# Attention and an MLP mixer in one kernel: value banks as two tiles, idle matmuls in the first steps, one weight load moved behind an input load

## The chip, the cores and the metric

One core of one Trainium2 chip runs the kernel. A core has TensorE (PE, matrix multiplication, writing into PSUM), VectorE (DVE), ScalarE (ACT), GpSimd (POOL) and SyncE (SP), which all work through their own instruction queues and wait for one another through semaphores. Sixteen DMA engines move data between the chip's memory (HBM) and the on-chip SBUF. PSUM has eight banks of 2 KB on each of 128 partitions. The metric is the device time of one execution in microseconds (us); lower is better.

## The reference

Batch 8, 12 heads, 448 rows, head size 64. First an attention with squared ReLU in place of softmax, then a mixer with a token part and a channel part.

```python
scores = scale * np.matmul(q, k.transpose(0, 1, 3, 2))
attn = np.maximum(scores, 0.0) ** 2 / S
x = (attn @ v).transpose(0, 2, 1, 3).reshape(B, S, H * D)      # 8 x 448 x 768
h = np.maximum(x.transpose(0, 2, 1) @ w_tok1, 0.0) @ w_tok2    # 448 -> 256 -> 448
u = x + h.transpose(0, 2, 1)
out = u + np.maximum(u @ w_ch1, 0.0) @ w_ch2                   # 768 -> 1536 -> 768
```

## The kernel before, in words

The work is cut into 24 groups, numbered i: four heads of one batch each, three groups to a batch (DB = 3). The order of all instructions is written out by hand.

For each group, `load_four` brings q, k and v by DMA from POOL's queue, with a cast to bf16: six DMAs of 112 KB (two for each of q, k, v). The pool for these has four buffers for each name. `transposes(i)` turns q and k with 56 small matmuls into a PSUM tile of two banks, which is copied to `qkT` (L148). `scores(i, c)`, c from 0 to 6, makes four matmuls of 64x64 by 448 columns into `sc_ps` (L159), and ACT writes their ReLU as `at` (L168). `square` squares `at` on DVE (L175). `values(i, cs)` adds up the products with v in `acc_ps` (L187). `values_out` scales the two halves of `acc_ps` into `xT` (L205 on DVE, and where `split` is set L201 on ACT for the second half).

Then the mixer: `x_back(i)` turns `xT` into `x_sb`, for the first six groups by matmuls into `x_ps` (L230) and a copy (L240, L241, L243), from group 6 on (XDMA = 6) by two DMA transposes on SP's queue (L223). `token1` multiplies `x_sb` with w_tok1 (`t_ps`, L252, ReLU L260), `token2` with w_tok2 (`h_ps`, L276), and DVE adds `xT` to give `uT_sb` (L284). `u_back` turns this back with DMA transposes on SP's queue (L306). `channel1` (L318, ReLU L325) and `channel2` (L357, sum L364) are cut into units that stand in a queue.

PSUM is shared by three pools: `ps_att` has two slots of two banks, taken in turn by `sc_ps` and by `qkT_ps` in the first groups ("att"); `ps_acc` has one slot of two banks ("acc") for `acc_ps`, later also for `qkT_ps` and `h_ps`; `ps_mm` has two slots of one bank ("bank") for everything else. One slot of two banks is one tile: instructions of two engines that use different halves of it are ordered one after the other.

The first three groups (steps 0 to 2) are a loop over c in which transposes, scores and values of neighbouring groups alternate (L438 to L465). Then comes a stretch for i = 3 written out by hand (L468 to L497), in which the first channel matmuls begin (`channel1_begin`, L336). From i = 4 on a loop (L500) does for each i: scores of group i, values of group i - 1, `x_back`, loads for group i + 3, transposes of group i + 1, `token1`, `token2`; in between, `fill(share)` takes channel units from the queue as a credit allows. From group 10 on, a load waits on POOL for the transposes of an earlier `x_sb` (`gate`, L518).

The loads stand in POOL's queue in the order in which they are written. Eight DMAs can be open at a time: POOL stops at a load until the one eight places before it has landed. The weights w_ch1 and w_ch2 come in two halves of 1152 KB each; the second half of w_ch2 is issued at i = 4, right after the loads of group 7 (L520).

Ahead of all this nine matmuls on zeros (`warm`, L420) run while the first inputs are on their way.

Of the kernel before, what the change touches and what calls it, by code (L numbers as in the profile page):

```python
# [9 lines left out]
FP32 = mybir.dt.float32  # L10
BF16 = mybir.dt.bfloat16
# [5 lines left out]
def kernel(  # L17
# [11 lines left out]
    nc = tc.nc  # L29
# [96 lines left out]

    def transposes(i, place="acc", split=False):
        sb = attn.tile([128, 2, 2, S], BF16, name="qkT")
        pool = {"acc": ps_acc, "att": ps_att}[place]
        ps = pool.tile([128, 2, 1024], BF16, tag=place, name="qkT_ps")  # L130
        for w in (1, 0) if i == 0 else (0, 1):
            src = raws.pop((i, "qk"[w]))
            for c in range(QC):
                at = w * S + c * 64
                for r in range(2):
                    h = slice(64 * r, 64 * (r + 1))
                    for g in range(2):
                        nc.tensor.matmul(  # L138
                            ps[64 * g : 64 * (g + 1), r, at : at + 64],
                            lhsT=src[h, g, c, :],  # L140
                            rhs=ident[h, h],
                            is_transpose=True,
                            start=True,
                            stop=True,
                            skip_group_check=True,
                        )
        for r in range(2):
            (nc.scalar.copy if split and r == 0 else nc.vector.tensor_copy)(  # L148
                sb[:, r].rearrange("n w t -> n (w t)"), ps[:, r, : 2 * S]
            )  # L150
        qkT[i] = sb

    def scores(i, c):
        sb = qkT[i]
# [17 lines left out]
    def square(keep=0):  # L172
        while len(squares) > keep:
            at = squares.pop(0)
            nc.vector.tensor_tensor(out=at, in0=at, in1=at, op=ALU.mult)  # L175

    def values(i, cs):
        v_raw = raws[i, "v"]
        if i not in accs:
            accs[i] = ps_acc.tile([128, 2, 512], FP32, tag="acc", name="acc_ps")  # L180
        ps = accs[i]
        for c in cs:
            at = at2.pop((i, c))
            for r in range(2):
                for g in range(2):
                    h = slice(64 * r, 64 * (r + 1))
                    nc.tensor.matmul(  # L187
                        ps[64 * g : 64 * (g + 1), r, :S],
                        lhsT=v_raw[h, g, c, :],
                        rhs=at[h, g, :],  # L190
                        start=(c == 0),
                        stop=(c == QC - 1),
                        skip_group_check=True,
                    )

    def values_out(i, split=False):
        b, d = divmod(i, DB)
        ps = accs.pop(i)
        for r in range(2):
            if split and r == 1:  # L200
                nc.scalar.activation(  # L201
                    xT[b % 2][:, 2 * d + r, :S], ps[:, r, :S], AF.Copy, scale=float(alpha2)
                )
                continue
            nc.vector.tensor_scalar(  # L205
                out=xT[b % 2][:, 2 * d + r, :S],
                in0=ps[:, r, :S],
                scalar1=float(alpha2),
                scalar2=None,
                op0=ALU.mult,  # L210
            )
# [2 lines left out]
    x_tiles, r1_tiles, uT_tiles = {}, {}, {}  # L214
    XDMA = 6

    def x_back(i, split=False):
        b, d = divmod(i, DB)
        x_sb = mix.tile([128, 2, 4, 128], BF16, name="x_sb")
        x_tiles[i] = x_sb  # L220
        if i >= XDMA:
            for r in range(2):
                nc.sync.dma_start_transpose(  # L223
                    out=x_sb[:, r], in_=xT[b % 2][:, 2 * d + r, :]
                )
            return
        ps = ps_mm.tile([128, 2, 512], BF16, tag="bank", name="x_ps")
        for r in range(2):
            for c in range(4):
                nc.tensor.matmul(  # L230
                    ps[:, r, c * 128 : (c + 1) * 128],
                    lhsT=xT[b % 2][:, 2 * d + r, c * 128 : (c + 1) * 128],
                    rhs=ident,
                    is_transpose=True,
                    start=True,
                    stop=True,
                    skip_group_check=True,
                )
        if split:
            nc.vector.tensor_copy(x_sb[:, 0].rearrange("n c d -> n (c d)"), ps[:, 0])  # L240
            nc.scalar.copy(x_sb[:, 1].rearrange("n c d -> n (c d)"), ps[:, 1])  # L241
            return
        nc.vector.tensor_copy(  # L243
            x_sb.rearrange("n r c d -> n (r c d)"), ps.rearrange("n r t -> n (r t)")
        )

# [16 lines left out]
    def token2(i, early=False, rs=(0, 1)):  # L263
        b, d = divmod(i, DB)
        if d == 0 and b % 2 == 0 and 0 in rs:
            uT_tiles[b // 2] = mix.tile([128, NP, 2 * S], BF16, name="uT_sb")
        r1 = r1_tiles[i]
        off = (b % 2) * S
        if early:
            parts = {r: ps_mm.tile([128, 512], FP32, tag="bank", name="h_ps1") for r in rs}  # L270
        else:
            both = ps_acc.tile([128, 2, 512], FP32, tag="acc", name="h_ps")
            parts = {r: both[:, r] for r in rs}
        for r in rs:
            for j in range(JC):
                nc.tensor.matmul(  # L276
                    parts[r][:, :S],
                    lhsT=r1[:, j, r * 128 : (r + 1) * 128],
                    rhs=wt2[:, j, :],
                    start=(j == 0),  # L280
                    stop=(j == JC - 1),
                )
        for r in rs:
            nc.vector.tensor_tensor(  # L284
                out=uT_tiles[b // 2][:, 2 * d + r, off : off + S],
                in0=parts[r][:, :S],
                in1=xT[b % 2][:, 2 * d + r, :S],
                op=ALU.add,
            )
        if 1 in rs:  # L290
            u_back(i)
# [34 lines left out]

    def channel1_begin():
        r2_tiles[0] = mix.tile([128, EC, 2 * S], BF16, name="r2_sb")
        first = ps_acc.tile([128, 2, 512], FP32, tag="acc", name="m1_ps2")
        for e in range(2):  # L330
            channel1_part(first, e, range(CC - 2))
        return first

    def channel1_part(ps, e, gs):
        for g in gs:
            nc.tensor.matmul(  # L336
                ps[:, e, :S],
                lhsT=wc1[:, g, e * 128 : (e + 1) * 128],
                rhs=uT_tiles[0][:, g, :S],
                start=(g == 0),  # L340
                stop=(g == CC - 1),
            )

    def channel1_end(ps):
        for e in range(2):
            channel1_part(ps, e, range(CC - 2, CC))
        nc.scalar.activation(r2_tiles[0][:, :2, :S], ps[:, :, :S], AF.Relu)

    def channel2(b, t, half):
        r2 = r2_tiles[b // 2]  # L350
# [67 lines left out]
    warm_ps = ps_mm.tile([128, 512], FP32, tag="bank", name="warm_ps")  # L418
    for i in range(9):
        nc.tensor.matmul(warm_ps, lhsT=warm[:, :128], rhs=warm, start=True, stop=True)  # L420
    for i in range(2):
        nc.vector.memset(xT[i][:, :, S:], 0.0)
    nc.vector.memset(wt1[:, 3, :], 0.0)
# [11 lines left out]
    load_four(3, "v")  # L435


    transposes(0, "acc", split=True)  # L438
    for i in range(DB):
        for c in range(QC):  # L440
            scores(i, c)
            square(keep=1)
            if c < 3 and i > 0:
                values(i - 1, (4 + c,))
                if c == 2:
                    values_out(i - 1, split=True)
            if c in (1, 2) and i > 1:
                token2(i - 2, early=True, rs=(c - 1,))
            if c == 3 and i == 0:
                transposes(1, "att")  # L450
            if c == 4 and i > 0:
                x_back(i - 1)
            if c == 5:
                if i > 0:
                    transposes(i + 1, "att", split=True)
                values(i, (0, 1))
            if c == 6:
                if i > 0:
                    token1(i - 1)
                values(i, (2, 3))  # L460
        if i == 1:
            load_four(4)
        if i == 2:
            load_four(5)
            load_wc1(1, 2)  # L465


    i = DB  # L468
# [2 lines left out]
    values_out(i - 1, split=True)  # L471
    scores(i, 0)
    token2(i - 2, early=True)
    x_back(i - 1, split=True)
    scores(i, 1)
    token1(i - 1)
    square(keep=1)
# [6 lines left out]
    scores(i, 4)  # L484
    channel1_end(first)
    square(keep=1)
    transposes(i + 1, "att", split=True)
    channel_work(0)
    scores(i, 5)
    square(keep=1)  # L490
# [9 lines left out]
    for i in range(DB + 1, ND + 2):  # L500
# [15 lines left out]
        if i + PRE < ND:  # L516
            if i - 1 >= XDMA:
                nc.gpsimd.tensor_copy(gate, x_tiles[i - 1][:1, 1, 3, 127:])  # L518
            load_four(i + PRE)
        if i == 4:  # L520
            load_wc2(1, 2)
        square()
        if not slow:
# [17 lines left out]
            if (i - 1) % DB == DB - 1:  # L541
                channel_work((i - 1) // DB)
        square()
        fill(1 / 3)
    while queue:
        queue.pop(0)[1]()

# [29 lines left out]
```

## Time and profile before

| | |
|---|---|
| median of 7 runs | 382.5 us (381.46 to 387.96) |
| the profiled execution | 382.44 us |
| its span, first to last instruction | 380.7 us |
| PE busy | 365.5 us (96%) |
| DVE busy | 203.8 us (54%) |
| ACT busy | 214.5 us (56%) |
| POOL busy | 98.0 us (26%) |
| read from HBM, written to it | 43.38 MB, 11.01 MB |
| mean granted TensorE clock | 0.982 of full |

The profile gives for each engine its busy time, in the whole span, in 40 slices of it or in any stretch that one asks for. The chain that ended last is followed back from the last instruction: at each step to what released it. A matmul's own duration contains the time that its data takes through the array; consecutive matmuls overlap. The granted clock is the share of TensorE's full speed that its throttle allowed. A DMA's time to landing runs from its issue to the moment its last packet is in place. The DMA share is the mean busy share of the sixteen engines, and packets of one engine can overlap, so that a share can be over 1.

### The profile page before, as it was taken

Reading aid. Unit: us, or ns where it says so; the run is one execution under the profiler, and the core shown is the slowest. Engines: PE = TensorE matmul, PEld = TensorE weight load, DVE = VectorE, ACT = ScalarE, POOL = GpSimd, SP = SyncE. Lnnn points to the kernel's source line nnn. Section 1 sums busy time; section 2 is a strip of 40 time slices with the busy share of each in tenths; the row PEclk is TensorE's granted clock in tenths of the full one; section 3 lists DMA queues with packets and bytes.
Section 4 is the critical chain, followed back from the end, with each engine's and each line's share of the span. In section 5 each row is a group of like instructions: output and inputs, shape, how many; then the busy total and the mean of one; then the engine's idle time right before and its main releaser. Section 6 shows DMA issues by size and latency. Waiting matters only on the chain.

```text
span 380.7 us, 10017 instructions
## 1 busy us (share of the span) xinstructions
PE 365.5 (96%) x4281; PEld 199.5 (52%) x4281; DVE 203.8 (54%) x372; ACT 214.5 (56%) x298; POOL 98.0 (26%) x176
## 2 busy tenths in 40 slices
PE   5887999989999999999999999999999999999995
PEld 2344455544555555555555655555545654555563
DVE  1776578853585575465555665556654755121022
ACT  4897788867455347654676347654676455411500
POOL 9873643313403303303303303303300000000000
PEclk9598999999999999999999999999999999999999
DMA  8999999997558889648646679568651343223024
GB/s 153 127 147 165 186 194 186 190 135 95 84 134 151 139 144 144 93 67 167 122 82 93 110 169 133 68 106 147 120 89 23 84 104 87 46 60 94 2 55 111
DMA packets 72013, 43.82 MB, mean 115 GB/s; under 512 B 46048, under 2 KB 68512, under 8 KB 71968
## 3 DMA queue, kind: packets, MB, share of 16 engines
q0 software_dynamic: 24416, 21.47, 40.3%
q1 hardware_dynamic: 47248, 21.28, 28.0%
q8 instruction: 33, 0.54, 0.6%
q10 hardware_dynamic: 304, 0.43, 0.4%
q14 instruction: 12, 0.10, 0.1%
HBM read 43.38 MB, written 11.01 MB: 143 GB/s over the span
## 4 chain that ended last, share of the span: by engine, by line
PE 87%; ACT 4%; DVE 3%; DMA 2%; POOL 2%; issue 1%; SPq 0%; POOLq 0%; ACTq 0%
PE m_ps L357 29%; PE m_ps L318 27%; PE sc_ps L159 9%; PE acc_ps L187 8%; PE t_ps L252 5%; PE h_ps L276 5%; PE qkT_ps L138 3%; ACT at L168 2%; DMA x_sb<-xT 1%; DVE qkT L148 1%; DMA wt<-in_moe_w_tok_dram 1%; DVE at L175 1%; POOL q_raw L83 1%; DVE uT_sb L284 1%; PE m_ps L336 1%
## 5 line engine op out<-in xcount | busy, mean ns | idle before, releaser
L168 ACT ACTIVATE at<-sc_ps 128x896 bf16<-128x896 f32 x168 | 144.9, 918 | 59.6 <-PE sc_ps L159 59.6
L318 PE MATMUL m_ps<-uT_sb,wc 128*128 128x448 bf16 x564 | 115.3, 353 | 0.0
L357 PE MATMUL m_ps<-wc,r_sb 128*128 128x384 bf16 x672 | 115.2, 326 | 0.0
L175 DVE TENSOR_TENSOR at<-at 128x896 bf16<-128x896 bf16 x168 | 96.9, 618 | 7.5 <-ACT at L168 7.5
L357 PEld LDWEIGHTS <-r_sb 128*128 128x128 bf16 x672 | 64.3, 98 | 45.7 <-issue 4.1
L325 ACT ACTIVATE r_sb<-m_ps 128x448 bf16<-128x448 f32 x94 | 51.2, 544 | 59.6 <-PE m_ps L318 59.1
L318 PEld LDWEIGHTS <-wc 128*128 128x128 bf16 x564 | 53.3, 98 | 49.8 <-issue 4.3
L364 DVE TENSOR_TENSOR out_sb<-m_ps,u_sb 128x384 f32<-128x384 f32 x56 | 31.0, 554 | 58.8 <-PE m_ps L357 58.8
L159 PE MATMUL sc_ps<-qkT 64*64 64x448 bf16 x672 | 54.9, 374 | 5.4 <-ACT at L168 2.7
L284 DVE TENSOR_TENSOR uT_sb<-h_ps,xT 128x448 bf16<-128x448 f32 x48 | 27.8, 619 | 48.3 <-PE h_ps L276 48.1
L205 DVE TENSOR_SCALAR xT<-acc_ps 128x448 bf16<-128x448 f32 x45 | 26.1, 619 | 30.4 <-PE acc_ps L187 30.4
L187 PE MATMUL acc_ps<-at,v_raw 64*64 64x448 bf16 x672 | 39.5, 362 | 0.0
L518 POOL COPY gate<-x_sb 1x1 bf16<-1x1 bf16 x14 | 3.0, 218 | 141.5 <-DMA x_sb<-xT 141.5
L148 DVE COPY qkT<-qkT_ps 128x896 bf16<-128x896 bf16 x44 | 25.6, 619 | 21.7 <-PE qkT_ps L138 16.7
L83 POOL DMA_DIRECT2D q_raw<-in_q_dram x48 | 28.9, 611 | 20.0 <-DMA wc<-in_moe_w_ch_dram 15.0
L159 PEld LDWEIGHTS <-qkT 64*64 64x64 bf16 x672 | 15.9, 107 | 33.8 <-issue 28.4
L83 POOL DMA_DIRECT2D v_raw<-in_v_dram x48 | 29.4, 632 | 11.6 <-DMA wc<-in_moe_w_ch_dram 6.0
L83 POOL DMA_DIRECT2D k_raw<-in_k_dram x46 | 28.0, 626 | 3.1 <-DMA q_raw<-in_q_dram 1.9
L252 PE MATMUL t_ps<-x_sb,wt 128*128 128x256 bf16 x192 | 25.5, 277 | 1.9 <-DMA x_sb<-xT 1.1
L187 PEld LDWEIGHTS <-v_raw 64*64 64x64 bf16 x672 | 20.0, 110 | 12.4 <-issue 1.8
L260 ACT ACTIVATE r_sb<-t_ps 128x512 bf16<-128x512 f32 x24 | 14.3, 597 | 20.1 <-PE t_ps L252 20.1
L252 PEld LDWEIGHTS <-wt 128*128 128x128 bf16 x192 | 18.6, 99 | 8.2 <-issue 1.9
(36 smaller groups left out, 109.5 us busy)
## 6 DMA issues: line engine op xcount, KB each, us to landing
out_dram<-out_sb SPq DMA_DIRECT2D x54, 192.0 KB, 2.8
q_raw<-in_q_dram POOLq DMA_DIRECT2D x48, 112.0 KB, 4.0
v_raw<-in_v_dram POOLq DMA_DIRECT2D x48, 112.0 KB, 5.1
k_raw<-in_k_dram POOLq DMA_DIRECT2D x46, 112.0 KB, 4.5
wc<-in_moe_w_ch_dram POOLq DMA_DIRECT2D x4, 1152.0 KB, 14.0
u_sb<-uT_sb SPq DMA_TRANSPOSE x48, 3.4
x_sb<-xT SPq DMA_TRANSPOSE x36, 2.5
k_first<-in_k_dram SPq DMA_DIRECT2D x1, 224.0 KB, 3.5
```

Source lines behind the costliest of these rows:

```text
L83: eng.dma_start(out=dst[64 * r : 64 * (r + 1)].rearrange("p g c d -> p g (c d)"), in_=src[b, h0 : h0 + 2].rearrange("g (p c) d -> p g (c d ...
L148: (nc.scalar.copy if split and r == 0 else nc.vector.tensor_copy)(sb[:, r].rearrange("n w t -> n (w t)"), ps[:, r, : 2 * S])
L159: nc.tensor.matmul(ps[64 * r : 64 * (r + 1), g, :S], lhsT=sb[h, r, 1, c * 64 : (c + 1) * 64], rhs=sb[h, r, 0, :], start=True, stop=True, s ...
L168: nc.scalar.activation(at, ps[:, :, :S], AF.Relu)
L175: nc.vector.tensor_tensor(out=at, in0=at, in1=at, op=ALU.mult)
L187: nc.tensor.matmul(ps[64 * g : 64 * (g + 1), r, :S], lhsT=v_raw[h, g, c, :], rhs=at[h, g, :], start=(c == 0), stop=(c == QC - 1), skip_gro ...
L252: nc.tensor.matmul(ps[:, j, :], lhsT=wt1[:, c, j * 128 : (j + 1) * 128], rhs=x_sb[:, :, c, :], start=(c == 0), stop=(c == 3),)
L284: nc.vector.tensor_tensor(out=uT_tiles[b // 2][:, 2 * d + r, off : off + S], in0=parts[r][:, :S], in1=xT[b % 2][:, 2 * d + r, :S], op=ALU.add,
L318: nc.tensor.matmul(ps[:, :S], lhsT=wc1[:, g, e * 128 : (e + 1) * 128], rhs=uT[:, g, off : off + S], start=(g == 0), stop=(g == CC - 1),)
L325: nc.scalar.activation(r2[:, e, off : off + S], ps[:, :S], AF.Relu)
L357: nc.tensor.matmul(ps[:, :HN], lhsT=r2[:, e, t * 128 : (t + 1) * 128], rhs=wc2[:, e, cols], start=(e == 0), stop=(e == EC - 1),)
L364: nc.vector.tensor_tensor(out=o[:, cols].rearrange("n (g d) -> n g d", d=128), in0=ps[:, :HN].rearrange("n (g d) -> n g d", d=128), in1=u_ ...
```

## The change

1. The `ps_acc` pool has two tags, `acc0` and `acc1`, of one bank each, in place of one of two banks. The values, `h_ps`, the first channel tile and the transposes in this pool take one tile of each, so that two engines can empty them at the same time. `channel1_end` evacuates each half by an instruction of its own.
2. Transposes that use `ps_att` are copied by one DVE instruction over both halves; before, ACT and DVE took one half each (or DVE both).
3. `x_back` in steps 1 and 2 is copied by ACT (`copy=nc.scalar.copy`). For group 2 it takes its PSUM from `acc0` and is copied by DVE in one piece.
4. `keep_clock(n)` issues n pairs of matmuls of 64x64 by 512 columns on zeros, whose result nobody reads: two pairs before the first transposes, three after, one or two behind most scores of step 0, and one behind each of the first four scores of step 1; 38 matmuls in all.
5. The second half of w_ch2 is issued at i = 5 instead of i = 4, behind the loads of group 8 (the ninth input).
6. The last `fill` of each iteration takes at least one unit while `slow` (i up to 6). This moves one unit of six channel matmuls from behind the values of group 6 to before the first scores of group 7. No other matmul of the steady loop changes its place.

```diff
-        pool = {"acc": ps_acc, "att": ps_att}[place]
-        ps = pool.tile([128, 2, 1024], BF16, tag=place, name="qkT_ps")
+        if place == "att":
+            both = ps_att.tile([128, 2, 1024], BF16, tag="att", name="qkT_ps")
+            parts = [both[:, r] for r in range(2)]
+        else:
+            parts = [ps_acc.tile([128, 1024], BF16, tag=f"acc{r}", name="qkT_ps1") for r in range(2)]
...
+        qkT[i] = sb
+        if place == "att":
+            nc.vector.tensor_copy(sb.rearrange("n r w t -> n r (w t)"), both[:, :, : 2 * S])
+            return
         for r in range(2):
             (nc.scalar.copy if split and r == 0 else nc.vector.tensor_copy)(
-                sb[:, r].rearrange("n w t -> n (w t)"), ps[:, r, : 2 * S]
-            )
-        qkT[i] = sb
+                sb[:, r].rearrange("n w t -> n (w t)"), parts[r][:, : 2 * S]
+            )
...
-            accs[i] = ps_acc.tile([128, 2, 512], FP32, tag="acc", name="acc_ps")
+            accs[i] = [ps_acc.tile([128, 512], FP32, tag=f"acc{r}", name="acc_ps") for r in range(2)]
...
-    def x_back(i, split=False):
+    def x_back(i, place="bank", copy=None):
...
-        ps = ps_mm.tile([128, 2, 512], BF16, tag="bank", name="x_ps")
+        pool = ps_mm if place == "bank" else ps_acc
+        ps = pool.tile([128, 2, 512], BF16, tag=place, name="x_ps")
...
-            both = ps_acc.tile([128, 2, 512], FP32, tag="acc", name="h_ps")
-            parts = {r: both[:, r] for r in rs}
+            parts = {r: ps_acc.tile([128, 512], FP32, tag=f"acc{r}", name="h_ps") for r in rs}
...
-        first = ps_acc.tile([128, 2, 512], FP32, tag="acc", name="m1_ps2")
+        first = [ps_acc.tile([128, 512], FP32, tag=f"acc{e}", name="m1_ps2") for e in range(2)]
...
-        nc.scalar.activation(r2_tiles[0][:, :2, :S], ps[:, :, :S], AF.Relu)
+            nc.scalar.activation(r2_tiles[0][:, e, :S], ps[e][:, :S], AF.Relu)
...
+    def keep_clock(n):
+
+        for m in range(n):
+            for r in range(2):
+                h = slice(64 * r, 64 * (r + 1))
+                nc.tensor.matmul(
+                    warm_ps[h, :], lhsT=warm[h, :64], rhs=warm[h, :],
+                    start=True, stop=True, skip_group_check=True,
+                )
...
+    keep_clock(2)
     transposes(0, "acc", split=True)
+    keep_clock(3)
     for i in range(DB):
         for c in range(QC):
             scores(i, c)
+            if i == 0:
+                keep_clock(0 if c == 3 else 1 if c > 4 else 2)
+            if i == 1 and c < 4:
+                keep_clock(1)
...
-                x_back(i - 1)
+                x_back(i - 1, copy=nc.scalar.copy)
...
-                    transposes(i + 1, "att", split=True)
+                    transposes(i + 1, "att")
...
-    x_back(i - 1, split=True)
+    x_back(i - 1, place="acc0")
...
-    transposes(i + 1, "att", split=True)
+    transposes(i + 1, "att")
...
-        if i == 4:
+        if i == 5:
             load_wc2(1, 2)
...
-        fill(1 / 3)
+        fill(1 / 3, least=1 if slow else 0)
```

## The prediction

> **What bounds the kernel now.** I read the page's slices first, then what TensorE (PE) waits for, then the chain that ended last, then stretches of a few microseconds.
>
> From the page: busy tenths, granted clock and DMA share in 40 slices of 9.5 us.
>
> ```profile
> PE   5887999989999999999999999999999999999995
> PEclk9598999999999999999999999999999999999999
> DMA  8999999997558889648646679568651343223024
> ```
>
> PE is saturated from the tenth slice on; from there only less PE work, or a wait taken away, could make the kernel faster. What is loose lies in the first 86 us: PE is at 5 to 8 tenths in the first four slices, and the clock is low in the second and fourth. In those same slices and up to 84 us the DMA row stands at 8 and 9.
>
> PE's waits over the whole span (total, times, longest):
>
> ```profile
> PE sc_ps L159 <- ACT at L168: 2.7, 7, 0.8
> PE sc_ps L159 <- DVE qkT L148: 1.6, 3, 0.8
> ...
> PE t_ps L252 <- DMA x_sb<-xT: 1.1, 1, 1.1
> ```
>
> All lie before 86 us. The last of them in time is the third, and the chain passes through it:
>
> ```profile
> 18.63 0.55 DVE xT L205
> 19.18 0.02 issue
> 19.20 0.54 ACT xT L201
> 19.75 2.44 ACT at L168 x3
> ...
> 79.90 5.06 DMA x_sb<-xT
> 85.10 1.03 PE t_ps L252 x8
> ```
>
> Two things to see. VectorE (DVE) and ScalarE (ACT) empty the two halves of one PSUM tile one after the other, and ACT's next scores queue behind that. And at 79.9 us the chain leaves the engines for a DMA transpose (x_sb of group 6), for which PE waits until 85.10. After that the chain is PE alone, back to back, to 376.7 us. So the end is 85.10 plus a fixed amount of PE work; **only what moves 85.10, or slows the PE behind it, moves the end.**
>
> Stretches around that point (PE, PEld, DVE, ACT, POOL busy, clock, DMA share, GB/s):
>
> ```profile
> 66.00:76.00 10.00, 9.50 (x165) 5.39 (x168) 8.50 (x17) 8.92 (x13) 3.39 (x6) 1.00 1.24 190
> 76.00:84.00 8.00, 8.00 (x121) 4.17 (x110) 5.46 (x10) 5.38 (x8) 1.18 (x2) 1.00 1.46 157
> 84.00:85.00 1.00, 0.04 (x1) 0.00 (x0) 0.00 (x0) 0.54 (x1) 0.00 (x0) 1.00 0.33 62
> 85.00:86.00 1.00, 0.90 (x9) 0.84 (x10) 0.00 (x0) 0.00 (x0) 0.93 (x3) 1.00 0.00 0
> ```
>
> The DMA engines are full to 84 and empty at 85: the transpose lands when the backlog of loads is gone. Issue to landing of the transposes, for u_sb issued at 65.6 and 66.9, x_sb at 78.6 and 79.9, and x_sb at 94.6 and 96.1 with no backlog:
>
> ```profile
> DMA to landing us min/median/max: 9.1/9.8/10.6
> ...
> DMA to landing us min/median/max: 5.1/5.5/5.9
> ...
> DMA to landing us min/median/max: 2.5/2.5/2.6
> ```
>
> **The change, part by part**, as the shift of PE's arrival at that transpose wait (84.04 now: 85.10 less 1.06).
>
> *First copies beside each other.* ACT copies qkT half 0 from 6.53 to 7.44, DVE starts half 1 only at 7.47 and ends at 8.09; the second score pair starts at 8.15. Side by side, all four start at 7.49: -0.66.
>
> *Idle matmuls.* 38 of 64x512, in pairs on opposite quadrants: 19 pairs. A warm-up matmul of 512 columns takes 0.43 us at the low clock (nine in 4.02), half of that at full: 0.22 to 0.43 per pair, double if a pair doesn't overlap. At full clock 4.2 us of them lie in PE's idle time up to 19 us, where each score waits 0.84 us for ACT; the four ahead of the first transposes (0.85 cold) end at 6.1, after k_raw's 5.8: +0.3, which the wait for ACT's copy hides only in part. In return scores stay at 0.37 us instead of 0.59, eight value matmuls at 0.57 instead of 0.96. I followed ACT's queue: four scores from 7.9, the fifth at 11.65, the sixth after the qkT copy at 12.75, then 13.7, and step 1's first at 14.65 against 16.25 now. The first two parts together: -1.6. If the clock isn't held, the pairs at 0.43 take it all back: 0.
>
> *Two value tiles.* ACT's xT no longer follows DVE's: idle 0.42, 0.67 and about 0.66 us in steps 1 to 3: -1.75.
>
> *Copies swapped.* In steps 1 and 2 ACT loses a qkT copy (0.91) and gets the whole x_sb. By 0.59 for 512 and 0.91 for 896 columns that is 1.0 us (bounds 0.9 and 1.2): +0.1 each. It now comes before scores 5 and 6, which share one PSUM slot while qkT_ps has the other, so score 6 waits for score 5's evacuation (0.45 each, formerly under the qkT copy): together +1.1. The whole qkT on DVE is 1.2 (two of 0.62; at least 1.15). In the group after step 2, x_sb was 0.42 + 0.04 + 0.59 serially, and is 0.69 on DVE: -0.36; its bank no longer waits for uT's: -0.34; the last qkT copy, 0.90 then 0.64, is 1.2, and PE's 0.45 behind it goes. Sum -1.15.
>
> *The extra channel unit after group 5* (six matmuls, 1.14 us, moved from three to two units behind the values of group 6): fills the 0.43 that PE waits for ACT at 75 us; the work is the same: -0.43.
>
> Sum: -1.6 -1.75 +1.1 -1.15 -0.43 = -3.8, so PE arrives at **80.2** (78.9 to 82.5).
>
> *Half acc tiles in the steady loop*: nothing; PE has no wait there, and DVE is at 5 tenths.
>
> *Ninth input ahead of the last weight.* On POOL's queue the six loads of group 8 go past one load of 1152 KB, the weight lands about 5 us later (78 to 79 against 73.6; first use 98.7 less the gain), group 8's keys at 72 instead of 76.7 (needed at 81.0, after the change 77). Group 9 no longer stands behind the weight's slot (5.4 us of POOL's wait). The bytes up to the gate that follows x_sb are the same six loads times three and two weights. POOL's issues up to there wait for landings, hardly for PE, so none of them starts earlier because PE is faster.
>
> **So when does x_sb of group 6 land?** The transpose is issued 2.7 us earlier (3.8 less the moved unit's 1.14), behind two u_sb transposes on SP's queue. The Trainium skill (DMA: Bandwidth & Descriptors, Queues, rings and completion order) says that each DMA engine takes the queues in turn, packet by packet: by that alone an earlier issue lands earlier, 2.7 us at most, and the total would be 382.44 - 2.7 = 379.7. The rows say that taking turns helps little where engines are full: loaded, a pair needs 9 to 11 us, and the four transposes (544 packets each in the trace, 2176) have more packets than the loads that will be queued when they start (by the order above some 390 of the weight and 860 of group 9), so they finish last whatever the order. The work until both queues are empty is the same, and so is its end: 84.5 to 85.0 now. The 157 GB/s of 76:84 against 190 before leave at most (1 - 157/190) x 8 = 1.4 us to recover; turns lost to the weight cost perhaps 0.5. Landing shift **-0.4**, between -1.4 and +0.5.
>
> **What PE does meanwhile** is wait from 80.2 to about 84.7: 4.5 us in place of 1.06. A wait that long has a price of its own; the one stretch of the trace that is like it and what follows (same columns):
>
> ```profile
> 26.60:30.05 3.45, 1.93 (x41) 1.06 (x40) 3.09 (x6) 2.78 (x5) 0.35 (x1) 0.94 1.15 202
> 30.05:33.45 3.40, 3.40 (x75) 1.96 (x71) 2.38 (x5) 2.30 (x3) 0.47 (x1) 0.56 1.27 171
> ```
>
> After 3.4 us with PE busy for 1.93 the clock is at half for 3.4 us of full work. The skill (TensorE: Matmul & The Clock Gate, Part 1) asks for a wholly idle free-running window of 3.4 us: a wait of 4.5 contains one in (4.5 - 3.4)/3.4, a third, of the phases, worth 0.7 on average. By the row a wait of 4.5 us is always enough. I take the row. Half clock then lasts from the restart to the end of the next full window, 2.8 to 6.2 us, and costs half of that, since the work there is PE-bound: 1.4 to 3.1, taken at **+2.0**.
>
> Sum on the profiled execution: 382.44 (its span 380.7 and 1.74 around it) - 0.4 + 2.0 = **384.0**, own range 383.0 to 385.6. That execution is 0.06 from the median of 382.5, so no correction. 0.3% (1.15 us) is about what can be told from no change.
>
> **Rivals.**
> *The gain is only swallowed* (x_sb lands at the same time, and the clock holds, or is not held early, so that PE arrives late and the wait stays short): 382.44 - 1.4 to +1.1, about 382.0. For it: the 1.06 us of slack. Against: the row at 26.6.
> *The transposes come through early*: faster. Issued at 76, x_sb lands by 82 because the freed POOL queue and better order empty the backlog early; the wait is then under 2 us, the clock holds, and the end comes 3 us earlier: 379.4 (378.4 to 381.2). It decides from a landing before about 82.5. For it: 157 GB/s in 76:84. Against: the full DMA row from 46 us.
> *Idle matmuls that don't overlap or stay cold*: PE is the bound up to 19 us; 19 x 0.43 = 8 us at worst, of which the idle 4 and the slack hide most: 382 to 384.
>
> **Numbers.** The stall with the clock lost 0.47, swallowed (with the cold matmuls) 0.29, early transposes 0.24. Range: the likeliest's upper end and a little for the phase, 385.8; down to 379.8, halfway into the fast case. Slower 0.47, same 0.29, faster 0.24.
>
> **What would show it.** No half clock between 9.6 and 19.8 us; ACT's and DVE's xT starting together; the wait of t_ps for x_sb grown from 1.1 to 4 us or more; its end still at 84 to 86; half clock right after it. A wait under 2 us ending before 82.5, or full clock after a wait of 4, makes the forecast wrong.

## The result and the profile after

The changed kernel takes 385.72 us (median of 15 runs, 380.94 to 387.36); the kernel before, measured beside it, 383.09 (36 runs). The ratio is 1.0058 with a 95% interval of 1.0036 to 1.0081: slower by 2.2 us, about twice the 1.15 us that the forecast took as telling from no change. The ratios here leave out the few executions that fell into a slower state, so that they differ a little from those of the medians (here 1.0069, or 2.6 us). The forecast of 384.0 is 1.7 us below the median; 385.72 lies at the upper edge of the range, inside it. The profiled execution took 386.48 us, with a span of 384.7 against 380.7 before and a mean granted clock of 0.989 against 0.982.

The slices of the page after (each now 9.6 us):

```profile
PE   7888999939998999999999999999999999999995
PEclk9999999988999999999999999999999999999999
DMA  8999999996467997388656687468561443224024
```

The first slices are what the change is for: PE goes from 5, 8, 8, 7 tenths to 7, 8, 8, 8, and the clock no longer drops there. But the ninth slice holds a new hole: PE at 3 tenths, with a reduced clock in it and in the next one.

PE's waits (total, times, longest) that answer to the three shown of before:

```profile
PE t_ps L255 <- DMA x_sb<-xT: 7.9, 2, 6.6
...
PE sc_ps L165 <- ACT at L174: 2.3, 6, 0.7
...
PE sc_ps L165 <- DVE qkT L152: 0.2, 1, 0.2
```

The wait for qkT fell from 1.6 to 0.2, that for `at` only from 2.7 to 2.3. The wait for the transposed `x_sb` grew from 1.1 to 7.9 us, 6.6 of it in one piece. Step 1's evacuations of the value banks, in the timeline (start, duration, engine):

```profile
16.87 0.62 DVE L211 TENSOR_SCALAR xT<-acc_ps 128x448 bf16<-128x448 f32 x1
16.95 0.59 ACT L207 ACTIVATE xT<-acc_ps 128x448 bf16<-128x448 f32 x1
```

They start 0.08 us apart; before, ACT followed DVE by 0.65 (18.55 and 19.20). The chain around the hole:

```profile
76.91 0.55 PE qkT_ps L141 x56
77.49 8.79 DMA x_sb<-xT
86.41 1.87 PE t_ps L255 x8
88.27 1.88 PE m_ps L320 x6
```

The second transpose of group 6 is issued 2.4 us earlier than before (77.49 against 79.90) and lands 1.3 us later. The first eight matmuls behind it take 1.87 us instead of 1.03, and the next six take 1.88. The stretches show why (PE, PEld, DVE, ACT, POOL busy, clock, DMA share, GB/s):

```profile
76.00:80.00 4.00, 3.77 (x79) 1.89 (x76) 2.86 (x6) 2.90 (x5) 0.00 (x0) 1.00 1.39 164
80.00:82.00 2.00, 0.00 (x0) 0.00 (x0) 0.00 (x0) 0.35 (x1) 0.00 (x0) 1.00 1.26 167
82.00:83.00 1.00, 0.00 (x0) 0.00 (x0) 0.00 (x0) 0.00 (x0) 0.00 (x0) 0.91 1.27 199
83.00:86.00 3.00, 0.00 (x0) 0.00 (x0) 0.00 (x0) 0.00 (x0) 0.00 (x0) 0.50 1.16 142
86.00:89.70 3.70, 3.29 (x13) 1.95 (x14) 0.00 (x0) 0.60 (x1) 3.32 (x7) 0.51 0.54 68
89.70:93.00 3.30, 3.30 (x24) 1.44 (x23) 1.82 (x4) 2.47 (x4) 0.42 (x1) 1.00 0.95 130
```

PE has nothing from 79.8 on, while the DMA engines stay full to 86. The clock falls to half at 82.8, which costs nothing while PE waits, and is still at half for the first 3.3 us of PE's work. Half of those 3.3 us is lost.

PE's timeline holds a second wait of this kind, for group 8's `x_sb`, which before had none:

```profile
86.41 1.87 PE L255 MATMUL t_ps<-x_sb,wt 128*128 128x256 bf16 x8 [6.64 <-DMA x_sb<-xT]
...
117.95 1.03 PE L255 MATMUL t_ps<-x_sb,wt 128*128 128x256 bf16 x8 [1.21 <-DMA x_sb<-xT]
```

So the span's +4.0 us is a restart 1.3 later (86.41 against 85.10), 1.6 lost to the clock, and 1.2 in the second wait.

### The profile page after: what moved, and what is told of

It reads as the page before. It is cut to its first block, busy times and chain, and to the rows that moved or that the text cites. A ratio compares the mean times of both kernels' runs of the same rounds, so it can differ in the third digit from the quotient of the medians.

```text
span 384.7 us, 10117 instructions
## 1 busy us (share of the span) xinstructions
PE 365.6 (95%) x4319; PEld 200.2 (52%) x4319; DVE 204.9 (53%) x369; ACT 213.2 (55%) x297; POOL 98.0 (25%) x176
## 4 chain that ended last, share of the span: by engine, by line
PE 86%; DMA 4%; DVE 4%; ACT 3%; POOL 2%; issue 1%; POOLq 0%; ACTq 0%
PE m_ps L359 28%; PE m_ps L320 28%; PE sc_ps L165 9%; PE acc_ps L193 8%; PE t_ps L255 6%; PE h_ps L278 5%; DMA x_sb<-xT 3%; PE qkT_ps L141 2%; ACT at L174 2%; DVE uT_sb L286 1%; DVE at L181 1%; POOL q_raw L83 1%; PE m_ps L338 1%; DMA wt<-in_moe_w_tok_dram 1%; ACT x_sb L246 1%
## 5 line engine op out<-in xcount | busy, mean ns | idle before, releaser
L165 PE MATMUL sc_ps<-qkT 64*64 64x448 bf16 x672 | 52.7, 360 | 2.9 <-ACT at L174 2.3
L193 PE MATMUL acc_ps<-at,v_raw 64*64 64x448 bf16 x672 | 38.6, 350 | 0.0
L155 DVE COPY qkT<-qkT_ps 128x896 bf16<-128x896 bf16 x39 | 22.5, 619 | 15.8 <-PE qkT_ps L141 15.8
L255 PEld LDWEIGHTS <-wt 128*128 128x128 bf16 x192 | 18.6, 99 | 14.6 <-DMA x_sb<-xT 7.1
```

The lines of the kernel that those rows point to most:

```text
L165: nc.tensor.matmul(ps[64 * r : 64 * (r + 1), g, :S], lhsT=sb[h, r, 1, c * 64 : (c + 1) * 64], rhs=sb[h, r, 0, :], start=True, stop=True, s ...
L193: nc.tensor.matmul(ps[r][64 * g : 64 * (g + 1), :S], lhsT=v_raw[h, g, c, :], rhs=at[h, g, :], start=(c == 0), stop=(c == QC - 1), skip_gro ...
L255: nc.tensor.matmul(ps[:, j, :], lhsT=wt1[:, c, j * 128 : (j + 1) * 128], rhs=x_sb[:, :, c, :], start=(c == 0), stop=(c == 3),)
```

## The experiments

My theory: the early gain is real and ends in a wait whose end doesn't move, and that wait, being long, costs the clock. Rivals: there was no gain to speak of; the order of the loads is what makes the transposes late; the clock is not what costs the time. Each kernel below was timed beside the kernel before; ratios are to that, with 95% intervals.

### Is it the order of the loads?

First the changed kernel with the last weight load back at its old place.

```diff
-        if i == 5:
+        if i == 4:
             load_wc2(1, 2)
```

> The changed kernel with the second half of w_ch2 issued at i = 4 again, ahead of group 8's loads. Theory (the total of queued transfers sets the landing of group 6's x_sb, in whatever order they stand): it lands at 84.5 to 86.5 us, PE waits 4 to 6.5 us, the clock falls, the time is that of the changed kernel within 1 us, 384.5 to 386.5. Rival (the new order of the loads makes the transposes late): they land at 82 or before, the wait is under 2.5 us, the time is 382.5 or less.

387.48 us, ratio 1.0109 (1.0064 to 1.0154). Not faster than the changed kernel, so the new order is not what makes the transposes late. In its chain (start, duration) the transposes still land at 84.4, with a wait of 4.5 us and the clock lost:

```profile
76.16 8.23 DMA x_sb<-xT
84.39 0.14 issue
84.53 1.87 PE t_ps L255 x8
```

The median is above my expectation and above the changed kernel's, but their intervals overlap. That the new order helps here is possible and not shown.

Then the same move alone, in the kernel before.

```diff
-        if i == 4:
+        if i == 5:
             load_wc2(1, 2)
```

> The kernel before with only the second half of w_ch2 moved to i = 5. Theory: PE comes to the wait at 84 as before, x_sb lands at 84.5 to 86.5, the wait is 0.5 to 2.5 us and too short for the clock to fall; 382 to 384. Rival (the order costs): the landing moves by 1.3 us or more and the clock falls after it, 384.5 or more.

382.75 us, ratio 1.001 (0.9981 to 1.0038). As expected: by itself it does nothing that can be measured.

### Was there a gain?

To take the wait away without touching the steps before it, group 6's `x_sb` is turned by PE, as that of groups 0 to 5 is, instead of by DMA. The first DMA transpose of this kind is then group 7's, and the gate on the loads begins one group later. This once in the changed kernel and once in the kernel before.

```diff
-    XDMA = 6
+    XDMA = 7
```

> The changed kernel with XDMA = 7: group 6 is turned back by PE (eight matmuls, 0.45 us) and a DVE copy, so no DMA transpose stands before its first product, and the gate on the loads begins one group later. Theory: the gain of the first steps (4.3 us at PE's arrival, 79.8 against 84.04) comes through with the 1.06 us of the old wait, less 0.45: 377 to 379, or up to 2 us more if group 7's transposes now meet group 10's loads. Rival (the early steps gained nothing that lasts): 381 or more.

> The kernel before with XDMA = 7. Theory: it loses its 1.06 us wait and pays 0.45 us, 381.5 to 382.5; the changed kernel with the same edit is 3 to 5 us below it. Rival: the two are within 1 us of each other.

In the changed kernel 379.79 us, ratio 0.9916 (0.9886 to 0.9946), a little above my expectation but clearly faster than both kernels. In the kernel before 383.69, ratio 1.0022 (1.0003 to 1.0041): about 1 us above what I expected, so there the remedy brings nothing. The start of group 6's `t_ps` in the two timelines, first with the change:

```profile
81.16 1.04 PE L255 MATMUL t_ps<-x_sb,wt 128*128 128x256 bf16 x8
```

and without it:

```profile
84.82 1.04 PE L252 MATMUL t_ps<-x_sb,wt 128*128 128x256 bf16 x8
```

With the DMA wait out of the way in both, the change is worth 3.7 us at this place and 3.9 us in the medians (379.79 against 383.69). The rival without a gain falls. In the kernel before, the wait of 1.06 us was traded for the transposes that PE now does itself: 84.82 is only 0.28 earlier than 85.10.

### What does the clock cost?

The changed kernel with 24 matmuls ahead of group 6's `token1` whose result nobody uses, so that PE is busy while it waits.

```diff
+        if i == 7:
+            idle = ps_mm.tile([128, 512], FP32, tag="bank", name="idle_ps")
+            for m in range(24):
+                nc.tensor.matmul(idle, lhsT=warm[:, :128], rhs=warm, start=True, stop=True)
         if 0 <= i - 1 < ND:
             token1(i - 1)
```

> The changed kernel with 24 idle matmuls of 128x512 (5.1 us at full clock) just before the first product of group 6 that waits for x_sb. Theory: x_sb lands as in the changed kernel (86 us), but the clock stays at full behind it, and the time is 1.4 to 2 us less than that of the changed kernel, about 383.8. Rival (the half clock is in the records but costs little): the time stays at 385 to 386.

382.63 us, ratio 1.0001 (0.9981 to 1.0021): 3.1 us less than the changed kernel by the medians, 2.2 by the two ratios, for 5.1 us of added PE work. PE's timeline and the stretches around it:

```profile
79.65 5.34 PE L555 MATMUL idle_ps<-warm 128*128 128x512 bf16 x23
84.83 1.04 PE L255 MATMUL t_ps<-x_sb,wt 128*128 128x256 bf16 x8
```

```profile
78.00:82.00 4.00, 3.95 (x20) 1.91 (x20) 1.71 (x4) 1.74 (x3) 0.00 (x0) 1.00 1.40 147
82.00:86.00 4.00, 4.00 (x24) 2.25 (x23) 0.00 (x0) 0.04 (x1) 2.26 (x5) 1.00 0.50 56
```

The clock stays at 1.00 and the time is that of the kernel before: the gain swallowed and nothing lost. I had expected 1.4 to 2 us; 2.2 to 3.1 is more than the 1.6 that the half clock costs in the profile. This execution has no second wait at group 8 either, and its transpose had landed by 83.7, about 1 us before PE was through with the idle matmuls, so the difference isn't all clock.

How much filling is needed? The same with 8 and with 14 of these matmuls.

```diff
-            for m in range(24):
+            for m in range(8):
```

> The changed kernel with 8 idle matmuls (1.7 us at 0.213 us each, by the 24 in 5.1 us) where the earlier kernel had 24. PE runs out of them at about 81.5, the transpose lands between 83.7 and 86.3, so the wait is 2.2 to 4.8 us. Theory (the row of the kernel before: PE busy for 1.93 of 3.45 us was followed by half clock): a wait of 2.2 us or more always loses the clock, time as the changed kernel, 384.5 to 386.5. Rival (only a window of 3.4 us that is wholly idle loses it): a wait under 3.4 us keeps the clock and one of 4.8 us loses it in four of ten phases, so mostly full clock and 382.5 to 383.5.

```diff
-            for m in range(24):
+            for m in range(14):
```

> The same with 14 idle matmuls, 3.0 us. PE runs out at about 82.8, the wait is 0.9 to 3.5 us. Theory: half clock where a window of 3.4 us has PE busy for about 1.9 us or less, that is for waits of 1.5 us or more in one window, so lost in some executions and held in others: 382.5 to 385.5. Rival (wholly idle window): the wait is too short to lose the clock, full clock throughout, 382.6 like the kernel with 24.

With 8: 382.63 us, ratio 1.0006 (0.9971 to 1.0041). With 14: 385.05, ratio 1.0041 (1.0011 to 1.0071). Neither theory foresaw that 14 would look worse than 8, and the two intervals overlap.

More telling are the single executions. One window of 3.4 us at half clock lowers the mean clock of a 382 us span by 0.5 x 3.4 / 382 = 0.0045. (The clock also falls at the very end, after PE's last work: in the changed kernel for the last 1.5 us of the span, which takes 0.002 off the mean. A mean of 0.996 or 0.997 therefore doesn't decide.) A mean of 0.996 or less was seen in 14 of 15 executions of the changed kernel, in all 6 with the old order of loads (0.990 or 0.991, two such windows), in 4 of 12 with 8 fillers, in 9 of 20 with 14, and in 1 of 22 with 24. With 14 the executions fall into two clusters, seven at 381.2 to 382.2 with full clock, and nine of the others at 385 to 387.5 with one window lost. The profiled one is of the first kind (wait 0.95 us):

```profile
83.86 1.03 PE L255 MATMUL t_ps<-x_sb,wt 128*128 128x256 bf16 x8 [0.95 <-DMA x_sb<-xT]
```

A partly filled wait was a gamble, and only the wait filled to its end was safe. That a wait of 2.2 us always loses the clock fits badly with 8 fillers, where 8 of 12 kept it; that only a wholly idle window loses it fits badly with 14, where 9 of 20 lost it in waits that I had put at 0.9 to 3.5 us.

Those executions have no trace that would give their waits, but the thirteen profiles say more. Where the half clock shows in them, ahead of the end, it lasts 3.41 us or two or three times that (82.83 to 89.66 in the changed kernel), so each trace can be laid out in windows of this length that begin where the clock changes. Two such windows of the changed kernel, two of the kernel before and two of the one with 14 fillers (columns as above):

```profile
79.41:82.83 3.42, 0.35 (x2) 0.00 (x0) 0.25 (x1) 0.54 (x1) 0.00 (x0) 1.00 1.12 150
82.83:86.24 3.41, 0.00 (x0) 0.00 (x0) 0.00 (x0) 0.00 (x0) 0.00 (x0) 0.50 1.09 135
...
26.22:29.63 3.41, 2.02 (x21) 0.91 (x21) 3.05 (x7) 2.74 (x5) 0.73 (x2) 1.00 1.14 204
29.63:33.05 3.42, 3.28 (x75) 2.06 (x75) 2.40 (x5) 2.72 (x4) 0.07 (x1) 0.50 1.25 169
...
82.35:85.76 3.41, 2.46 (x17) 1.36 (x15) 0.00 (x0) 0.60 (x1) 1.92 (x4) 1.00 0.40 50
85.76:89.18 3.42, 3.42 (x25) 1.58 (x24) 2.12 (x4) 2.70 (x4) 1.81 (x4) 1.00 1.04 138
```

The busy time of the first window in each pair goes with the clock of the second. Over all profiles eight windows at full clock were followed by half clock; PE was busy in them for 0 to 2.02 us. Every window of the recorded clock with 2.04 us or more was followed by full clock, and so was one with 1.94. So no wholly idle window is needed (the changed kernel's had PE busy for 0.35 us): about 1.4 us of idle time in one window was enough. By this a wait of 2.2 us loses the clock or not according to where the edge of a window cuts it, and one of 4.5 us leaves over 2 us in one window wherever the edge falls. (By my estimate from these figures a wait of 2.2 us would keep the clock in about one of six phases; so many of the 8 in 12 that kept it probably waited less, which isn't shown.)

### Parts of the change, with the wait out of the way

With XDMA at 7, first without the idle matmuls of the first steps:

```diff
-        for m in range(n):
+        for m in range(0):
```

> The changed kernel with XDMA = 7 and none of the idle matmuls (the PSUM tiles, copies and orders of the change stay). Theory: the full clock in steps 0 and 1 is worth about 1.6 us of the early gain, so it is 1 to 2.5 us slower than with them, 378.5 to 381. Rival (ACT sets the pace of these steps whatever the clock): within 0.5 us of the run with them.

379.46 us, ratio 0.9907 (0.9872 to 0.9941): a miss, since the time is the same as with them. (The 1.6 us that I gave them is the forecast's sum for two parts; 0.66 of it are the first copies.) In the profile the half clock is back in the first steps, and group 6's `t_ps` starts later than in the kernel that has the idle matmuls (81.16, above):

```profile
82.03 1.04 PE L255 MATMUL t_ps<-x_sb,wt 128*128 128x256 bf16 x8
```

So they bring 0.9 us at this place. By the end even that is gone: the kernel with them has a wait that this one lacks, at 110.68 us, for a DVE sum:

```profile
PE t_ps L255 <- DVE out_sb L366: 0.8, 1, 0.8
```

Then with the weight load back at i = 4 (the edit of the first experiment, with XDMA at 7):

> The changed kernel with XDMA = 7 and the second half of w_ch2 at i = 4 again. Theory: with PE some 4 us earlier the inputs of group 8, behind the weight, come late (keys landed at 76.7 us in the kernel before, needed at about 77): 0 to 2 us slower than with the new order. Rival (the order never mattered): within 0.5 us of it.

380.01 us, ratio 0.9925 (0.99 to 0.9951): 0.2 from the kernel with the new order. The order of these loads cannot be measured here either.

### Is it the backlog of loads?

In the changed kernel the last weight is put behind the gate, the POOL instruction that waits for group 6's `x_sb`. Its 1152 KB are then out of the DMA engines' way until the transposes have landed.

```diff
             if i - 1 >= XDMA:
                 nc.gpsimd.tensor_copy(gate, x_tiles[i - 1][:1, 1, 3, 127:])
+            if i == 7:
+                load_wc2(1, 2)
             load_four(i + PRE)
-        if i == 5:
-            load_wc2(1, 2)
```

> The changed kernel with the second half of w_ch2 (1152 KB) issued behind the gate that waits for group 6's x_sb, so that some 6 us of transfers are taken out of the backlog ahead of the transposes. Theory (backlog): x_sb lands at 79.5 to 82, PE waits under 2.5 us, the clock holds, the gain of the first steps comes through: 378.5 to 381. Rival (the landing is set by SP's own queue or by the transposes' own time): it still lands at 84 or later and the time is 383.5 or more.

379.89 us, ratio 0.9935 (0.9908 to 0.9962). The chain, then the stretches:

```profile
77.56 4.99 DMA x_sb<-xT
82.55 0.14 issue
82.69 1.03 PE t_ps L255 x8
```

```profile
80.00:82.00 2.00, 1.48 (x8) 0.58 (x6) 1.50 (x3) 1.35 (x3) 0.00 (x0) 1.00 0.35 67
82.00:83.00 1.00, 0.31 (x3) 0.32 (x4) 0.00 (x0) 0.06 (x1) 0.34 (x2) 1.00 0.00 0
```

Issued at the same moment as in the changed kernel (77.56 against 77.49), the second transpose now takes 4.99 us instead of 8.79, and the DMA share is down to 0.35 at 80 us. The landing at 82.6 is later than the 79.5 to 82 I had expected, but far from the 84 or later of the rival. The clock holds in this profile and, by the mean clock, in 19 of the 22 executions.

The wait of 1.2 us is short for a second reason, which the edit did not make: PE comes late. Its waits, and the start of the one for a weight in the timeline:

```profile
PE t_ps L255 <- DMA x_sb<-xT: 2.8, 3, 1.2
...
PE m_ps L320 <- DMA wc<-in_moe_w_ch_dram: 1.5, 1, 1.5
...
53.49 1.31 PE L320 MATMUL m_ps<-uT_sb,wc 128*128 128x448 bf16 x6 [1.47 <-DMA wc<-in_moe_w_ch_dram]
```

This is the second half of w_ch1, needed 29 us before the moved load is issued (82.84). PE stands before the transposes at 81.5 instead of 79.8; without the 1.5 us of delay the wait would have been up to 2.7 us. The profiled execution (381.78 us) is accordingly among the slower ones of this kernel.

The other profiles point the same way. Five of them have the new order of loads and still turn group 6 by DMA (the changed kernel, those with 8, 14 and 24 fillers, and the kernel before with the new order). In them the last weight is issued at 65.0, 65.1, 66.3, 66.9 and 67.7 us, and `x_sb` lands at 83.7, 83.7, 85.1, 86.3 and 86.5: 18.6 to 19.3 us later each time, while the second transpose is issued between 76.0 and 79.9. The landing goes with the state of the loads, not with the issue of the transposes. Why the loads run up to 2.7 us apart was not tested.

Last, both remedies together (XDMA at 7, and the weight load at i = 7 as here):

> The changed kernel with x_sb of group 6 turned by PE (XDMA = 7) and the last weight behind the gate at i = 7. If the wait for the transposes is all that stood in the way, each of the two remedies alone has taken it and both together give what each gave: 379.5 to 380.5. If the weight behind the gate also empties the DMA engines earlier for what follows, it adds up: 377.5 to 379. If the weight, then used some 10 us after it is issued, becomes the next wait, it is slower than either alone: 380.5 to 382.

379.43 us, ratio 0.9922 (0.9892 to 0.9953). They don't add up: each alone takes the wait away, and there is only one wait to take. The waits of PE in this profile show none for the weight. The smallest edit of the lot, XDMA = 7 alone, gives the same time.

## Why the prediction was right or wrong

**PE's arrival at the wait: right.** 80.2 was predicted, in the profile it is 86.41 - 6.64 = 79.8. XDMA = 7, where nothing hides the gain, agrees: 3.7 us against the 3.8 of the sum.

**Its parts: mostly as sized, with one term left out.** "The first two parts together: -1.6": step 1's first scores reach ACT at 14.56, with 14.65 forecast and 16.25 before. Of the 1.6, 0.66 was put down to the first copies, which leaves 0.94 for the idle matmuls; with XDMA = 7 they are worth 0.9 us at group 6, though nothing that can be measured at the end. The value tiles did what was said (ACT and DVE 0.08 us apart). At step 2's `xT` on ACT the gain is 2.10 us (27.55 before, 25.45 after), where the terms up to there make 2.14. It is by the next `h_ps` on PE (34.62 and 31.98) that the gain is larger than the sum, 2.64 against 2.25, and that is nearly all of the surplus. Between the two lies the half clock of 29.63 to 33.05 of the kernel before, which the forecast read for its rule on waits and gave no term in the gain. The profile of the kernel before with XDMA = 7 has full clock there and needs 6.11 us from the one mark to the other instead of 7.07. So 0.96 us came from a loss that the kernel before has in some executions only, and the other terms of this stretch brought about 0.5 less than put down. That the sum came out right is partly luck.

**The landing: the mechanism right, the bound too narrow.** "Landing shift -0.4, between -1.4 and +0.5" rests on a backlog that ends when it ends, however early the transpose is issued. That held: `x_sb` lands 18.6 to 19.3 us after the issue of the last weight, whenever the transpose is issued, and with one weight taken from the backlog it landed at 82.6. But the landing itself varies more between executions than I allowed: 83.7, 84.4 and 86.3 in three profiles (24 fillers, old order of loads, changed kernel) with the same bytes to be moved, so +1.3 in the profiled execution is outside the bound. One execution of the kernel before could not show that spread.

**The clock: right in kind, a little less in size.** "By the row a wait of 4.5 us is always enough. I take the row": the clock was lost in nearly every execution of the changed kernel, and the windows of all profiles bear the row out. The term of +2.0 measured 1.6 in the profile. The rule of the Trainium skill (TensorE: Matmul & The Clock Gate, Part 1) of one idle window of 3.4 us has the length right, but taken as a wholly idle window, as the forecast read it, it does not fit: PE was busy for 0.35 us in the window that cost the changed kernel the clock, and for 2.02 us in the one at 26.22 us of before. The measurement decides.

**What was not foreseen: group 8.** The second wait (1.2 us in the profile) is in no step of the forecast; the landing rows of before, 2.5 us for group 7's transposes, gave no reason for it. With the landing (+1.3 instead of -0.4, a difference of 1.7), this and the clock (-0.4) make up the distance of the profiled execution from 384.0: 1.7 + 1.2 - 0.4 = 2.5, and 386.48 - 384.0 = 2.5. So the profiled execution lies outside the range, and the median just inside.

**The rivals.** "The gain is only swallowed" is about what happens once the wait is filled (382.63 with 24 fillers, 382.0 forecast). "The transposes come through early" is about what happens once the backlog is shorter (379.89, with 379.4 forecast; it landed at 82.6, close to the point at which that rival was said to decide). Both needed a further edit; in the changed kernel as it stands neither came about, except perhaps in its one execution at full clock (380.94).

## What to carry to other kernels

Follow an early gain to the next wait and ask what ends that wait: if it is a DMA behind a full backlog, arriving earlier only makes the wait longer. A longer wait isn't free: here it cost the TensorE clock for the work behind it, which turned a swallowed gain into a loss. Then look for what is in that backlog and not needed yet, or for a way round the queue: here one number (XDMA = 7), or one load moved by two iterations, made the slower kernel 0.6 to 0.8% faster than the one before.

## What the runs showed of the hardware

- The clock changes in steps of 3.41 us. In the changed kernel it fell at 82.8, some 3.1 us after PE ran dry, stayed at half through a further 3.6 us of waiting and then for 3.3 us of work, and came back at 89.7. In the thirteen profiles it fell after steps in which PE was busy for at most 2.02 of 3.41 us, and came back after steps with 2.86 us or more, not after those with 2.66 or less.
- The clock on record can miss the start of a profile. In the kernel before with XDMA = 7 it reads 1.00 from 9.6 to 16.4 us, yet four scores take 0.59 us there, as at the half clock on record in the kernel before, against 0.38 later.
- A DMA transpose of the same size, issued when the backlog of loads was gone, mostly landed after 2.4 to 2.5 us. But from group 8 on, in each of the thirteen profiles, three to seven of the pairs for `x_sb` held one that took 3.1 to 4.5 us; one is group 8 of the changed kernel, 113.46 to 117.81. The chain of the changed kernel there:

```profile
113.46 4.36 DMA x_sb<-xT
117.81 0.14 issue
117.95 1.03 PE t_ps L255 x8
```

What causes it was not tested and stays open; it is worth up to 1.2 us here, and may be part of why some executions at full clock are as late as those that lost it.
